# S2 and S4 by pairs of even and of odd chunks, P3's chunks in another order, and A22's third small sum in two halves

## The chip, the cores and the metric

The kernel runs on one core of a Trainium2 chip. The metric is the device time of one launch in microseconds; lower is better. The core has five engines: TensorE (PE) for matmuls, VectorE (DVE), ScalarE (ACT) and GpSimd (POOL) for elementwise work, and SyncE (SP), which here only issues DMAs. POOL issues DMAs too, among them those that add what they carry to what lies at the destination. Each engine works through its own instructions in their order, and waits for the others at semaphores.

## The reference

A causal convolution of 7 taps over 8 sequences of 4096 tokens and 192 channels, with softmaxed weights for each of 8 heads, and after it a feed-forward layer with 2048 hidden channels and a hard-swish:

```python
h = x @ w_in                      # x: 32768 x 192, w_in: 192 x 2048
relu6 = np.clip(h + 3.0, 0.0, 6.0)
g = h * relu6 / 6.0
return (g @ w_out).astype(np.float32)   # w_out: 2048 x 192
```

## The kernel before

The 32768 tokens are taken in 32 blocks of 1024, in two halves of 512. Block 0 is done directly. Blocks 1 to 31 run in a loop of `first_layer` and `second_layer`; what follows is about these.

**First layer.** The hidden channels are 16 chunks of 128; with the two token halves, `g` holds for each of 8 chunk numbers c four tiles of 128 x 512: A11 and A22 (written in the first eight steps, n = 0 to 7) and A21 and A12 (n = 8 to 15). In each step TensorE makes h from a split of inputs and weights in three parts (line 511), ScalarE scales it (L523) and makes the clipped factor (L302), and VectorE multiplies (L306, the "gate").

**Second layer.** `g @ w_out` is a product of 2 x 2 blocks, done with seven products P1 to P7 in place of eight, after sums of the A blocks: S1 = A21 + A22, S2 = S1 - A11, S3 = A11 - A21, S4 = A12 - S2. Four of the seven are split once more in the same way into "small" products, on quarters of the chunks and tokens: x11 and x12 are the even and the odd chunks of the first 256 tokens, x21 and x22 those of the last 256. Their sums are `small_sums` (L600; forms 1 to 4), into the tiles `shared` (for A11), `sums4` (a tile z, for A22), `sums2` (a tile z, for A12) and `s5` (for S1, in the place of A22).

Several sums lie in place of what they come from: S1 lies in A21, S2 in A11, and S4 in the tile s of S3. So each has to wait until the last reader of the old content is through:

- S3 (`third_sum`, `g_sums`, L414): by chunk pairs 0 to 3. Pair 0 on VectorE at n == 9, pair 1 on POOL at n == 11, pairs 2 and 3 on VectorE at the start of the second layer.
- S1 (`add_pair`, L568): a DMA from POOL's queue adds A22 to A21, one pair of chunks after its third_sum.
- S2 (L458 onto g): VectorE subtracts A11 from S1, in place of A11. Its readers are P1 and the small products of P1, which read the even chunks early and the odd chunks of the last 256 tokens last.
- S4 (`negative`, which calls `difference`): ScalarE writes -S2 into the chunk's place in s (L571), and a DMA from POOL's queue adds A12 (L568). The old content, S3, is read by P7; the new one by P3.

TensorE runs four streams of matmuls side by side, each with 32 output rows. Every stream is a list of parts with a cost: 2 for a matmul of 512 columns, 1 for one of 256, 80 in all. `put` and `do` give each matmul and each job of the other engines a time on this scale, and all of them are sorted by it. That sets the order in every engine's queue; it is written out by hand, and nothing is reordered later:

```python
def put(j, cost, fn):
    streams[j].append((clock[j], fn))
    clock[j] += cost

def do(t, fn, *args, **kw):
    streams[3].append((t - 0.5, lambda: fn(*args, **kw)))
```

P7 reads s from 4 to 44, P6 reads S2 from 44 to 60, P3 reads s from 64 to 80, chunk by chunk. In the last block P3 runs by halves of the tokens (`plain_by_halves`), each over all eight chunks.

Between the small products ScalarE copies partial results out of PSUM or within it (lines 740 to 745 from `level_two`, L647 for the rest). Three of those within it are C2, D2 (both copies of B2) and the copies between `a[second]` and `a[fourth]`. `last_sum` negates a small sum of A12 on ScalarE (L571 into z) and adds to it by DMA; `fold_with` adds the parts of P1 on VectorE, and a copy of 96 rows (L647) then puts P1 where P6 is added to it.

Of the kernel before, what the change touches and what calls it, by code (L numbers as in the profile page):

```python
# [8 lines left out]
ALU = mybir.AluOpType  # L9
# [16 lines left out]
def kernel(  # L26
# [8 lines left out]
    nc = tc.nc  # L35
# [10 lines left out]
    D2 = P // 2  # L46
# [8 lines left out]
    NP = NC // 2  # L55
# [32 lines left out]
    for base, dma in ((0, nc.scalar), (D2, nc.sync)):  # L88
        dma.dma_start(
            out=w_sb[base : base + D2],  # L90
            in_=weight.unsqueeze(1).to_broadcast([H, GJ, KC]),
# [126 lines left out]
    for n in range(AHEAD):  # L218
# [8 lines left out]
        out=e_sb[:], in0=w_sb[:], in1=mx[:].to_broadcast([P, KC]), op=ALU.subtract  # L227
# [46 lines left out]
    A11, A21, A12, A22 = (g4[:, :, j] for j in range(4))  # L274
    S2, S1, S4 = A11, A21, A12
# [25 lines left out]
    def relu(r6, h):  # L301
        nc.scalar.activation(r6, h, ACT.Relu, bias=half[:], scale=1.0 / 6.0)  # L302

    def gate(g_, h):

        nc.vector.scalar_tensor_tensor(  # L306
            out=g_, in0=g_, scalar=1.0, in1=h, op0=ALU.min, op1=ALU.mult
        )
# [46 lines left out]
    every = range(NP)  # L355
# [48 lines left out]
    def g_sums(engine, which, slots, width):  # L404

        forms = {
            3: (S3, A11, A21, ALU.subtract),
            2: (S2, S1, A11, ALU.subtract), 4: (S3, A12, S2, ALU.subtract),
        }
        for n in which:  # L410
            o, a, b, op = forms[n]
            for p in slots[::width]:
                r = slice(p, p + width)
                engine.tensor_tensor(out=o[:, r], in0=a[:, r], in1=b[:, r], op=op)  # L414
# [42 lines left out]
    def add(out, x, y, op=ALU.add):  # L457
        nc.vector.tensor_tensor(out=out, in0=x, in1=y, op=op)  # L458
# [13 lines left out]
    def r32(ap):  # L472
        return ap.bitcast(F32R)
# [16 lines left out]
    y_own, y_other, pools, sums4 = [], [None], [], []  # L490
# [8 lines left out]
    def first_layer(i, jobs):  # L499

        slots = {}

        def both(n):
            return psum[:, 2 * slots[n] : 2 * slots[n] + 2]

        def mms(n, part, start=False, stop=False):
            group, c = divmod(n, NP)
            for s in range(K3):
                for k in range(2):
                    r = slice(k * D2, (k + 1) * D2)  # L510
                    nc.tensor.matmul(  # L511
                        out=psum[:, 2 * slots[n] + k], lhsT=r32(w_in_parts[part][r, c, s]),
                        rhs=r32(y_other[0][r, part, s] if group else y_own[part][r, s]),
                        start=start and s == 0, stop=stop and s == K3 - 1,
                        skip_group_check=True,
                    )

        def begin(n):
            slots[n] = free_slots.pop(0)
            mms(n, HIGH, start=True)  # L520
            mms(n, LOW)
            if n + 1 < count:
                nc.scalar.mul(both(n), both(n), 4097.0)  # L523
            else:
                lower, upper = (psum[:, 2 * slots[n] + k] for k in range(2))
                nc.scalar.mul(lower, lower, 4097.0)
                nc.vector.tensor_scalar(
                    out=upper, in0=upper, scalar1=4097.0, scalar2=None, op0=ALU.mult
                )

        def end(n):
            group, c = divmod(n, NP)
            mms(n, MIX, stop=True)
            to = g4[:, c, 1:3] if group else g4[:, c, 0::3]
            relu(to, both(n))
            gate(to, both(n))
            free_slots.append(slots[n])

        count = 2 * NP
        begin(0)  # L540
        begin(1)
        for job in jobs.get(-1, ()):
            job()
        for n in range(count):
            if n == count - 3:
                begin(n + 2)
            end(n)
            if n < count - 3:
                begin(n + 2)
            for job in jobs.get(n, ()):  # L550
                job()
            if n < NP and n % 2:
                small_sums(shared, A11, (3, 2, 4), nc.gpsimd, every[n - 1 : n + 1])
            if n == NP - 1:
                sums4[:] = [pools[0].tile([P, NP, N], F32, name="z4", tag="own")]
                nc.sync.dma_start(out=four_parts(sums4[0])[0], in_=four_parts(A22)[2])
            if n == NP + 1:
                third_sum(0, nc.vector)
                add_pair(0)
                adding(four_parts(sums4[0])[0], four_parts(A22)[3])  # L560
                small_sums(sums4[0], A22, (3,), nc.gpsimd)
            if n == NP + 3:
                third_sum(1)
                add_pair(1)
                small_sums(sums4[0], A22, (2,), nc.gpsimd)

    def adding(out, x):
        nc.gpsimd.dma_start(out=out, in_=x, accum_op=ALU.add)  # L568
# [5 lines left out]
    def pair_of(p):  # L574
        return slice(2 * p, 2 * p + 2)

    def third_sum(p, engine=nc.gpsimd):
        g_sums(engine, (3,), every[pair_of(p)], 2)

    def add_pair(p):  # L580
        adding(S1[:, pair_of(p)], A22[:, pair_of(p)])

    TH = N // 2
    halves = slice(0, TH), slice(TH, N)

    def four_parts(x):
        return [x[:, c::2, t] for t in halves for c in range(2)]

    def small_sums(to, x, which, engine=nc.gpsimd, r=every):

        r = slice(r[0], r[-1] + 1)
        x11, x12, x21, x22 = four_parts(x[:, r])
        s1, s2, s3, s4 = four_parts(to[:, r])
        forms = {
            1: (s1, x21, x22, ALU.add), 2: (s2, x22, s3, ALU.subtract),
            3: (s3, x11, x21, ALU.subtract), 4: (s4, x12, s2, ALU.subtract),
        }
        for n in which:
            o, p, q, op = forms[n]
            engine.tensor_tensor(out=o, in0=p, in1=q, op=op)  # L600
# [17 lines left out]
    def second_layer(i, between):  # L618
        last = i + 1 == NB
        ours = [free_slots.pop(0) for _ in range(3)]  # L620
        x_, b, y_, c, a, _ = (psum[:, 2 * n + k] for n in ours for k in range(2))
# [3 lines left out]
        s5 = A22  # L625
        copy = nc.scalar.copy
        m = slice(0, DH)
        lo, hi = halves
# [7 lines left out]
        A2, E2, C2, B2, D2 = f[first, lo], f[second, hi], h[first, lo], h[second, hi], h[third, hi]  # L636
# [9 lines left out]
        def do(t, fn, *args, **kw):  # L646
            streams[3].append((t - 0.5, lambda: fn(*args, **kw)))  # L647
# [7 lines left out]
        def plain(j, bank, n, q, chunks, start=False):  # L655
            x, w = prod[n]
            x = S3 if x is None else x
            for k, ch in enumerate(chunks):
                put(j, 2, lambda ch=ch, k=k: matmul(
                    j, bank[rows(j)], w_out[:, ch, w, q * QS : (q + 1) * QS], x[:, ch],  # L660
                    start and k == 0,
                ))
# [27 lines left out]

        def plain_by_halves(j, n, q, t):
            w = prod[n][1]
            for ch in every:
                put(j, 1, lambda ch=ch: matmul(
                    j, ends[t][rows(j), halves[t]], w_out[:, ch, w, q * QS : (q + 1) * QS],
                    S3[:, ch, halves[t]], ch == 0,
                ))
# [25 lines left out]
        def p3(q):  # L723
            if last:
                plain_by_halves(q, 3, q, 0)
                plain_by_halves(q, 3, q, 1)
            else:
                plain(q, b, 3, q, every)

        class Fourth:  # L730
            def __getitem__(self, at):
# [82 lines left out]
        do(25.5, copy, out=p1[third], in_=b[second])  # L814
        do(20, copy, out=B2, in_=A2)
        do(31.9, copy, out=C2, in_=B2)
        do(32.2, copy, out=D2, in_=B2)
        do(12, copy, out=a[second], in_=a[fourth])
        do(34, copy, out=a[fourth], in_=a[second])
        do(40, lambda: copy(out=p2(second, hi), in_=C2))  # L820
# [13 lines left out]
        do(7, small_sums, sums2, A12, (3, 2), nc.vector)  # L834
        do(7, small_sums, sums4[0], A22, (4,), nc.vector)
        do(7, small_sums, sums2, A12, (1,), nc.vector)
        for r, t, when in (
            (slice(0, 4), lo, 28.5), (slice(4, 6), lo, 28.6),
            (slice(0, 4), hi, 32.5), (slice(4, 6), hi, 32.6),
        ):  # L840
            do(when, lambda r=r, t=t: add(S2[:, r, t], S1[:, r, t], A11[:, r, t], ALU.subtract))
        do(32, tiles)
        do(36.03, fold_with, p1)
        do(36.07, small_sums, s5, S1, (3,), nc.vector)
        do(36.1, g_sums, nc.vector, (2,), every[6:], 2)
        do(36.2, small_sums, s5, S1, (2,), nc.vector)
        do(36.05, fold_with, p4, 2)
        do(40 if last else 38.7, copy, out=b[m], in_=p1)
        do(21, last_sum, sums2, A12)
        do(36.3, small_sums, s5, S1, (1, 4), nc.vector)  # L850
        for n, t in zip(range(0, NP, 2), (36.3, 39, 41, 48.3)):
            do(t, negative, slice(n, n + 2))
        do(56.5, lambda: copy(out=late["p7"], in_=c[m]))
        do(60.2, lambda: add(late["u3"], b[m], late["p7"]))
        for t in halves:
# [82 lines left out]
    with tc.manual_schedule():  # L938
# [4 lines left out]
            out=c_sb[:], in0=e_sb[:], in1=sm[:].to_broadcast([P, KC]), op=ALU.mult  # L943
# [14 lines left out]
        b = take()  # L958
        for _ in range(3):

            nc.tensor.matmul(
                out=psum[:, b], lhsT=zeros[:, 0:P], rhs=zeros[:], start=True, stop=True
# [58 lines left out]
        n = 3  # L1021
# [146 lines left out]
```

## Time and profile before

| what | value |
|---|---|
| median of 3 runs | 2228.58 us (2228.41 to 2228.99) |
| profiled execution | 2228.83 us |
| its span, first to last instruction | 2227.1 us |
| granted TensorE clock, of full speed | 0.999 |
| busy: TensorE, VectorE, ScalarE, POOL | 2214.7, 2022.1, 1740.9, 1180.5 us |
| second layer's matmuls on s (x3024) | 721.6 us busy, 3.1 us of idle before them, 2.8 of it for the DMA into s |
| ScalarE's wait for VectorE ahead of the negation of z (x31) | 46.9 us |

A row of a timeline gives the start in us from the start of the span, the duration in us, the engine, the line, the operation, what it writes and reads by the program's names with the shape, how many instructions are merged in the row, and in brackets the idle time of the engine before it and what ended it. A row of the chain gives start, duration and what: the chain is followed back from the last instruction to whatever released it. A row of the view of one line gives the count and then the minimum, median and maximum of the duration in ns.

### The profile page before, as it was taken

How to read it: one execution, taken by the hardware profiler on the slowest of the kernel's cores; microseconds unless marked ns; L12 is line 12 of the kernel's file. 1: busy time of each engine (PE TensorE's matmuls, PEld its weight loads, DVE VectorE, ACT ScalarE, POOL GpSimd, SP SyncE). 2: the span in 40 equal slices, each digit the busy share in tenths (PEclk: the TensorE clock that was granted, in tenths of full speed). 3: DMA queues.
4: the chain of work that ended last, by engine and by line, in shares of the span. 5: the costliest groups of instructions: out<-in, count | busy, mean ns of one | idle time of the engine just before them, and what ended most of it. 6: DMA issues, size and time to landing. Idle time of an engine off the chain costs nothing.

```text
span 2227.1 us, 55364 instructions
## 1 busy us (share of the span) xinstructions
PE 2214.7 (99%) x22984; PEld 1461.4 (66%) x22984; DVE 2022.1 (91%) x2014; ACT 1740.9 (78%) x2391; POOL 1180.5 (53%) x1002
## 2 busy tenths in 40 slices
PE   9999999999999999999999999999999999999998
PEld 5466666667666666666676666666666666667765
DVE  8899999999899999999999999999999999999977
ACT  7478787787877878877878778787778787787875
POOL 2456545565544556445555546554456545565544
PEclk9999999999999999999999999999999999999999
DMA  6277788777778777787777887777877788777776
GB/s 157 61 134 137 145 150 150 135 140 146 147 138 157 135 142 147 143 157 131 139 146 148 143 151 135 146 143 141 159 130 139 143 150 151 139 137 143 137 141 113
DMA packets 353308, 313.20 MB, mean 141 GB/s; under 512 B 212480, under 2 KB 265216, under 8 KB 353056
## 3 DMA queue, kind: packets, MB, share of 16 engines
q0 software_dynamic: 114976, 234.46, 58.8%
q1 hardware_dynamic: 236840, 74.93, 16.8%
q8 instruction: 180, 2.95, 0.6%
q14 instruction: 72, 0.59, 0.1%
q10 hardware_dynamic: 1240, 0.27, 0.1%
HBM read 31.72 MB, written 25.17 MB: 26 GB/s over the span
## 4 chain that ended last, share of the span: by engine, by line
PE 92%; DMA 4%; ACT 2%; DVE 1%; issue 0%; SPq 0%; DVEq 0%; ACTq 0%
PE psum L511 46%; PE psum L650 43%; DMA s<-g 4%; PE psum L296 2%; PE psum L341 2%; ACT s L571 1%; ACT psum L647 0%; DMA x<-in_x_dram 0%; ACT shared L823 0%; ACT psum L740 0%; ACT y_own L476 0%; ACT shared L822 0%; DVE z L600 0%; DVE g L306 0%; DVE shared L458 0%
## 5 line engine op out<-in xcount | busy, mean ns | idle before, releaser
L650 PE MATMUL psum<-g,w_out 128*32 128x512 f32 (+1 forms) x5968 | 827.5, 503 | 0.6 <-ACT psum L647 0.6
L650 PE MATMUL psum<-s,w_out 128*32 128x512 f32 (+1 forms) x3024 | 721.6, 586 | 3.1 <-DMA s<-g 2.8
L306 DVE SCALAR_TENSOR_TENSOR g<-g,psum 128x1024 f32<-128x1024 f32 (+1 forms) x528 | 618.9, 1186 | 102.9 <-ACT g L302 102.6
L302 ACT ACTIVATE g<-psum,half 128x1024 f32<-128x1024 f32 (+1 forms) x528 | 565.4, 1088 | 6.0 <-PE psum L511 5.2
L511 PE MATMUL psum<-y_own,w_in 64*128 64x512 f32 x4464 | 523.3, 389 | 0.0
L511 PE MATMUL psum<-y_other,w_in 64*128 64x512 f32 x4464 | 516.0, 386 | 0.0
L523 ACT ACTIVATE psum<-psum 128x1024 f32<-128x1024 f32 x465 | 468.7, 1008 | 48.0 <-PE psum L511 45.3
L650 PEld LDWEIGHTS psum<-g,w_out 128*32 128x32 f32 x5968 | 337.4, 110 | 246.0 <-issue 110.6
L511 PEld LDWEIGHTS psum<-y_own,w_in 64*128 64x128 f32 x4464 | 413.5, 184 | 117.7 <-issue 26.0
L511 PEld LDWEIGHTS psum<-y_other,w_in 64*128 64x128 f32 x4464 | 418.1, 184 | 87.8
L600 POOL TENSOR_TENSOR shared<-g,shared 128x256 f32<-128x256 f32 x248 | 356.7, 1438 | 80.2 <-DVE g L306 48.6
L1058 DVE SCALAR_TENSOR_TENSOR y<-x,c_sb,y 128x1536 f32<-128x1536 f32 x186 | 335.4, 1803 | 1.5 <-ACT y L1056 1.3
L650 PE MATMUL psum<-g,w_s 128*32 128x256 f32 x1488 | 283.2, 380 | 0.3 <-ACT shared L744 0.3
L568 POOL DMA_DIRECT2D s<-g x124 | 148.5, 1199 | 231.4 <-ACT s L571 223.1
L650 PE MATMUL psum<-z,w_s 128*32 128x256 f32 x992 | 232.4, 380 | 0.0
L650 PEld LDWEIGHTS psum<-s,w_out 128*32 128x32 f32 x3024 | 193.8, 109 | 58.5 <-issue 15.9
L650 PE MATMUL psum<-z,w_out 128*32 128x256 f32 x992 | 231.4, 380 | 0.0
L568 POOL DMA_DIRECT2D g<-g x124 | 150.4, 1276 | 151.0 <-PE psum L511 86.7
L600 POOL TENSOR_TENSOR shared<-g 128x256 f32<-128x256 f32 x124 | 91.9, 741 | 167.9 <-DVE g L306 167.9
L650 PEld LDWEIGHTS psum<-g,w_s 128*32 128x32 f32 x1488 | 134.5, 110 | 61.6 <-ACT shared L744 14.4
L647 ACT COPY psum<-psum 32x512 f32<-32x512 f32 (+1 forms) x186 | 82.9, 446 | 117.0 <-PE psum L650 113.1
L266 POOL DMA_DIRECT2D y_other<-y_own x90 | 48.1, 534 | 237.8 <-PE psum L650 237.8
(116 smaller groups left out, 2975.2 us busy)
## 6 DMA issues: line engine op xcount, KB each, us to landing
y_other<-y_own POOLq DMA_DIRECT2D x180, 384.0 KB, 8.0
g<-g POOLq DMA_DIRECT2D x124, 512.0 KB, 5.3
s<-g POOLq DMA_DIRECT2D x124, 512.0 KB, 7.8
z<-g POOLq DMA_DIRECT2D x62, 512.0 KB, 7.4
out_dram<-shared SPq DMA_DIRECT2D x378, 64.0 KB, 4.5
x<-in_x_dram SPq DMA_DIRECT2D x53, 388.5 KB, 5.6
z<-g SPq DMA_DIRECT2D x31, 512.0 KB, 3.3
stage<-in_moe_w_in_dram SPq DMA_DIRECT2D x16, 192.0 KB, 4.7
```

Of the source, the lines that this page charges most:

```text
L266: dma.dma_start(out=to[D2:P], in_=part[0:D2])
L296: nc.tensor.matmul(out=psum[:, b], lhsT=w[r], rhs=src, start=start, stop=stop, skip_group_check=onto,)
L302: nc.scalar.activation(r6, h, ACT.Relu, bias=half[:], scale=1.0 / 6.0)
L306: nc.vector.scalar_tensor_tensor(out=g_, in0=g_, scalar=1.0, in1=h, op0=ALU.min, op1=ALU.mult)
L341: lambda p=p: nc.tensor.matmul(out=bank[j * QS : (j + 1) * QS, tokens], lhsT=w_out[:, p, w, cols], rhs=x[:, p, tokens], start=(first and p ...
L511: nc.tensor.matmul(out=psum[:, 2 * slots[n] + k], lhsT=r32(w_in_parts[part][r, c, s]), rhs=r32(y_other[0][r, part, s] if group else y_own[ ...
L523: nc.scalar.mul(both(n), both(n), 4097.0)
L568: nc.gpsimd.dma_start(out=out, in_=x, accum_op=ALU.add)
L600: engine.tensor_tensor(out=o, in0=p, in1=q, op=op)
L647: streams[3].append((t - 0.5, lambda: fn(*args, **kw)))
L650: nc.tensor.matmul(out=out, lhsT=w, rhs=x, start=start, stop=True, tile_position=(0, j * QS), skip_group_check=True,)
L1058: jobs.append(lambda k=k: nc.vector.scalar_tensor_tensor(out=y[:], in0=x[:, :, k : k + N], scalar=c_sb[:, k : k + 1], in1=y[:], op0=ALU.mu ...
```

## The change

- A22's third small sum (form 3 of `sums4`), which POOL did in one at n == 9, is done in two halves: chunks 0 to 3 at n == 7, chunks 4 to 7 at n == 9. At n == 11 POOL's second small sum goes ahead of `add_pair(1)`.
- S2 was made in five sums: chunks 0 to 3 and 4 to 5 by token halves, chunks 6 and 7 whole. Now it is made in four, by the chunk pairs 0 2, 4 6, 1 3 and 5 7 in this order, each over all tokens.
- S4's four negations with their DMAs go by the pairs 0 2, 1 3, 4 6, 5 7 in place of 0 1, 2 3, 4 5, 6 7, at 30.5, 36.3, 42.1 and 44.2 in place of 36.3, 39, 41 and 48.3. So in ScalarE's queue the first negation now stands ahead of copy C2 (31.9).
- The copy D2 goes from 32.2 to 45.
- P3 takes the chunks in the order 0 2 1 3 4 6 5 7, in the last block too.
- The third sum of `s5` goes from 36.07 to 36.15, behind S2's last pair.

The number of matmuls and their order by size and stream are the same.

```diff
             if n == NP - 1:
                 sums4[:] = [pools[0].tile([P, NP, N], F32, name="z4", tag="own")]
                 nc.sync.dma_start(out=four_parts(sums4[0])[0], in_=four_parts(A22)[2])
+                small_sums(sums4[0], A22, (3,), nc.gpsimd, every[:4])
             if n == NP + 1:
                 third_sum(0, nc.vector)
                 add_pair(0)
                 adding(four_parts(sums4[0])[0], four_parts(A22)[3])
-                small_sums(sums4[0], A22, (3,), nc.gpsimd)
+                small_sums(sums4[0], A22, (3,), nc.gpsimd, every[4:])
             if n == NP + 3:
                 third_sum(1)
+                small_sums(sums4[0], A22, (2,), nc.gpsimd)
                 add_pair(1)
-                small_sums(sums4[0], A22, (2,), nc.gpsimd)
...
+    in_fours = 0, 2, 1, 3, 4, 6, 5, 7
+    chunk_pairs = [slice(n, n + 3, 2) for n in (0, 1, 4, 5)]
...
-            for ch in every:
+            for ch in in_fours:
                 put(j, 1, lambda ch=ch: matmul(
                     j, ends[t][rows(j), halves[t]], w_out[:, ch, w, q * QS : (q + 1) * QS],
...
-                plain(q, b, 3, q, every)
+                plain(q, b, 3, q, in_fours)
...
-        do(32.2, copy, out=D2, in_=B2)
+        do(45, copy, out=D2, in_=B2)
...
-        for r, t, when in (
-            (slice(0, 4), lo, 28.5), (slice(4, 6), lo, 28.6),
-            (slice(0, 4), hi, 32.5), (slice(4, 6), hi, 32.6),
-        ):
-            do(when, lambda r=r, t=t: add(S2[:, r, t], S1[:, r, t], A11[:, r, t], ALU.subtract))
+        for r, when in zip(chunk_pairs, (28.5, 32.5, 28.6, 36.1)):
+            do(when, lambda r=r: add(S2[:, r], S1[:, r], A11[:, r], ALU.subtract))
         do(32, tiles)
         do(36.03, fold_with, p1)
-        do(36.07, small_sums, s5, S1, (3,), nc.vector)
-        do(36.1, g_sums, nc.vector, (2,), every[6:], 2)
+        do(36.15, small_sums, s5, S1, (3,), nc.vector)
         do(36.2, small_sums, s5, S1, (2,), nc.vector)
...
-        for n, t in zip(range(0, NP, 2), (36.3, 39, 41, 48.3)):
-            do(t, negative, slice(n, n + 2))
+        for r, t in zip(chunk_pairs, (30.5, 36.3, 42.1, 44.2)):
+            do(t, negative, r)
```

## The prediction

> **What bounds the kernel now.** I read the page first, for the busiest engine and for the chain that ended last, then that chain in order of time, because only it says which waits move the end.
>
> ```profile
> PE 2214.7 (99%) x22984; PEld 1461.4 (66%) x22984; DVE 2022.1 (91%) x2014; ACT 1740.9 (78%) x2391; POOL 1180.5 (53%) x1002
> PE 92%; DMA 4%; ACT 2%; DVE 1%; issue 0%; SPq 0%; DVEq 0%; ACTq 0%
> 99.82 32.93 PE psum L511 x288
> ...
> 413.30 1.21 DVE s L414
> ...
> 419.55 0.37 ACT shared L744
> ...
> 419.97 22.68 PE psum L650 x167
> ...
> 1112.75 1.06 ACT s L571
> ...
> 1114.11 9.17 DMA s<-g
> ...
> 1123.32 1.93 PE psum L650 x16
> 1125.25 32.97 PE psum L511 x288
> 1158.22 35.21 PE psum L650 x289
> ...
> 2150.28 32.97 PE psum L511 x288
> ```
>
> TensorE is busy for 99% of the span. One block of the loop is 288 matmuls of the first layer (L511, 32.97 us) and then the second layer (L650). A block without a visible wait takes 32.97 + 35.21 = 68.18 us. From the first L511 stretch (99.82) to the last (2150.28) lie 30 blocks in 2050.46 us, 68.35 each: so all visible waits of these 30 blocks are worth 30 x 68.35 - 30 x 68.18 = 5.1 us. The chain names two kinds. Mostly it is the last chunk pair of S4, which P3 waits for: ScalarE writes -S2 (L571, 1112.75), POOL's DMA adds A12 and lands 9.17 us after its issue at 1114.11, and sixteen matmuls later the block ends. Once, at 413 to 420, it is VectorE's third sum, then ScalarE's copy L744. What remains inside the 35.21 us shows only beside the engines of one block. Below is the block whose second layer starts at 1089.7; a part of a stream that costs 1 there (I call it a unit) lasts about 0.43 us: ScalarE's copies of units 16 and 20, both waiting for TensorE, start at 1096.89 and 1098.60.
>
> ```profile
> 1101.98 0.38 PE L650 MATMUL psum<-z,w_s 128*32 128x256 f32 x1
> ...
> 1102.31 0.41 PE L650 MATMUL psum<-g,w_s 128*32 128x256 f32 x2
> 1105.83 0.40 PE L650 MATMUL psum<-z,w_out 128*32 128x256 f32 x1
> 1109.09 4.24 PE L650 MATMUL psum<-g,w_out 128*32 128x256 f32 x40
> 1096.89 0.72 ACT L742 COPY psum<-psum 32x256 f32<-32x256 f32 x2 [1.20 <-PE psum L650]
> 1098.60 0.34 ACT L647 COPY psum<-psum 32x256 f32<-32x256 f32 x1 [1.00 <-PE psum L650]
> 1100.42 1.06 ACT L571 ACTIVATE z<-z 128x1024 f32<-128x1024 f32 x1 [1.48 <-DVE z L600]
> 1101.89 0.36 ACT L744 COPY shared<-psum 32x256 f32<-32x256 f32 x1
> 1102.88 0.37 ACT L743 COPY z<-psum 32x256 f32<-32x256 f32 x1
> 1105.07 1.28 ACT L647 COPY psum<-psum 32x256 f32<-32x256 f32 x3
> 1107.04 1.05 ACT L571 ACTIVATE s<-g 128x1024 f32<-128x1024 f32 x1
> 1108.12 0.59 ACT L647 COPY psum<-z 96x512 f32<-96x512 f32 x1
> ...
> 1093.08 3.78 DVE L414 TENSOR_TENSOR s<-g 128x1024 f32<-128x1024 f32 x2
> 1099.16 2.36 DVE L600 TENSOR_TENSOR z<-g,z 128x1024 f32<-128x1024 f32 x2
> 1102.58 3.56 DVE L458 TENSOR_TENSOR g<-g 128x1024 f32<-128x1024 f32 x4
> ...
> 1085.02 3.35 POOL L600 TENSOR_TENSOR z<-g 128x1024 f32<-128x1024 f32 x1
> 1087.38 3.34 POOL L414 TENSOR_TENSOR s<-g 128x1024 f32<-128x1024 f32 x1
> 1091.02 1.19 POOL L568 DMA_DIRECT2D g<-g  x1 [0.30 <-POOL s L414]
> 1091.77 2.86 POOL L600 TENSOR_TENSOR z<-g,z 128x1024 f32<-128x1024 f32 x1
> ...
> L414 DVE TENSOR_TENSOR s<-g x93: 1210/1225/3420, 124.6 to 2189.1; 128x1024 f32<-128x1024 f32 x93
> ```
>
> This is the part the change works on. VectorE's pair of third sums (L414) takes 3.78 us, though a sum of this shape takes 1.22 us at the median of 93 and 1.21 at least. The first of the two is the one held up: 3.78 - 1.14 - 1.22 leaves some 1.4 us, and POOL's second small sum ends at 1091.77 + 2.86 = 1094.63, inside it. Everything behind it on VectorE is late by the same 1.4 us, and so ScalarE idles 1.48 us at 1100.42 for a sum of VectorE, with all its copies queued behind. Two of these copies hold TensorE: L744 ends at 1102.25 and TensorE goes on at 1102.31; of the three L647 copies behind 1105.07 the first two (C2 and D2) are of the size that takes 0.34 at 1098.60, so D2 ends near 1105.78, and TensorE goes on at 1105.83.
>
> **Part one, POOL's sums.** The third small sum of A22 now runs half at n == 7 and half after add_pair(0), and the second small sum goes ahead of add_pair(1). What is left behind 1085.02 is half a sum, POOL's third_sum and the second sum. With whole durations this is 1085.02 + 1.7 + 3.34 + 2.86 = 1092.9; with the pitch of the rows (1087.38 - 1085.02 = 2.36 for a whole one) it is 1085.02 + 1.2 + 2.36 + 2.36 = 1090.9, to which the overlap with the DMA issue may add one. Both lie ahead of VectorE's 1093.08. So the pair takes 1.22 + 1.14 and ends 1.4 us earlier (1095.4), and the sum for which ScalarE waits ends at about 1099.0. Queued behind the moved second sum is add_pair(1): issued 1 to 2 us later, it lands near 1098, ahead of the first S2 sum that reads it, at 1101.2.
>
> ```profile
> 1077.61 3.01 POOL L600 TENSOR_TENSOR shared<-g,shared 128x256 f32<-128x256 f32 x2 [0.37 <-POOL shared L600]
> 1081.59 1.23 DVE L414 TENSOR_TENSOR s<-g 128x1024 f32<-128x1024 f32 x1
> 1084.41 1.22 DVE L306 SCALAR_TENSOR_TENSOR g<-g,psum 128x1024 f32<-128x1024 f32 x1 [0.46 <-ACT g L302]
> ```
>
> The moved half starts at 1080.62, when POOL's last row of the first layer ends, and ends 1.2 to 1.7 us later, at 1081.8 to 1082.3; VectorE wants its first third_sum at 1081.59. If that one is held up like the pair above, it loses 0.2 to 0.7 us, and 0.46 us of idle two sums later takes it up. Bounds: 0 to 0.24 us in 31 blocks, 0 to 7 us; I take 0, since TensorE is two chunks behind there. The Trainium skill (SBUF — State Buffer, Who interferes with whom) has it that a VectorE instruction with two SBUF inputs and a GpSimd instruction reading SBUF lock each other out for the whole instruction, the earlier one winning. The held pair of L414 agrees; by that rule the moved half does hold up this sum in every block, and the total would lie in the same 0 to 7 us.
>
> **Part two, ScalarE's queue.** Today the chain from L743 to the end of D2 is 1102.88 to 1105.78. L743 waits for unit 28, which by the rows of units 16 and 20 is served at 1098.60 + 8 x 0.43 = 1102.03. With the last sum's negation at 99.0 to 100.1 and L744, L647 behind it (0.39 + 0.39 + 0.6), ScalarE is free at 1101.5: L744 no longer holds TensorE, and L743 starts at 1102.03, 0.85 us earlier. Then comes the added wait: the first S4 negation (30.5) stands ahead of copy C2 (31.9), for 1.08 us; D2 (0.37) leaves. So C2 ends 0.85 - 0.71 = 0.14 us earlier, and TensorE, for which C2 is now the last, goes on 0.08 to 0.14 us earlier at this place. Take 0.1: 31 x 0.1 = -3.1 us. The bounds are wide: without any gain on VectorE it would be +0.71 per block, and with both holds gone (0.33 us of delay at 1102.31, after 1101.98 by the pace, and as much again at 1105.83) about -0.65. Queued behind the negation are also L745, the second negation and the 96-row copy that P6 waits for: 1108.12 becomes 1107.98, ahead of TensorE's 1109.09 at P6, so its cover stays 0.4 us.
>
> **Part three, S2 by pairs.** Five sums become four of 1.22 us: what was 3.56 + 1.22 is now 4.88, nothing to speak of. The order is what counts. The second sum, chunks 4 and 6, now needs add_pair(2) and add_pair(3); these issue 1.4 us earlier, with their third sums.
>
> ```profile
> 1096.44 2.43 POOL L568 DMA_DIRECT2D g<-g  x2 [1.82 <-DVE s L414]
> DMA to landing us min/median/max: 5.1/6.2/7.3
> DMA to landing us min/median/max: 5.0/7.8/9.6
> ```
>
> The first landing row is of these two, so the later one, issued near 1097.2, lands at 1104.5, and after the change near 1103.1. VectorE reaches this sum at 1102.4, waits 0.7 us, and ends chunks 1 and 3 at 1103.1 + 1.22 + 1.14 = 1105.5. ScalarE wants them for the second negation at 1106.9. The cover is 1.4 us; a landing 9.6 us after its issue, the most of any S4 addition (the second landing row), uses it up and costs 0.9. I put +1.2 us over the kernel for a few late blocks; bounds 0 and 31 x 0.9 = 28. The third sum of s5, now behind S2's last pair, only changes places with it.
>
> **Part four, S4 and P3.** The last negation moves from 1112.75 to about 1110.8 and its DMA issues near 1112.1, 2 us earlier; the three before it move 2 to 3 us earlier too. Even at 9.6 us to landing it is there at 1121.7, and P3 wants it, as the sixth chunk now instead of the seventh of 0 to 7 but at the same unit 76, at about 1122.9 (1123.32, where TensorE now goes on, less a wait of some tenths). So the waits on S4 go, and with the earlier VectorE the one at 413 too: -5.1 us. What is late next is C2 (part two). In the last block P3 runs by halves and wants the last pair at unit 70:
>
> ```profile
> 2214.63 0.59 PE L650 MATMUL psum<-g,w_out 128*32 128x256 f32 x2
> 2216.23 0.42 PE L650 MATMUL psum<-s,w_out 128*32 128x256 f32 x3 [1.00 <-DMA s<-g]
> ```
>
> The next step was due 0.2 us after 2214.63; 2216.23 is 1.4 us late, and 2 us earlier covers it: -1.4 us.
>
> **The sum.** -5.1 - 1.4 - 3.1 + 1.2 = -8.4 us. The profiled execution took 2228.83 us (span 2227.1); the median of the runs, 2228.58, is 0.25 lower. That gives 2220.4; I say 2220.5, -0.36%. A difference under 0.2% (4.5 us) can't be told from none by a measurement of this kernel.
>
> **Rivals.** First, slower: the queue is paid and the gain does not come. If POOL's second sum still lies over VectorE's pair, ScalarE's chain starts as late as now and C2 ends 0.71 us later in each block: +22 - 6.5 = +15.5 us, 2244. It decides from the point where POOL's sum ends after about 1093.7, 0.6 us into VectorE's pair; against it stands 1090.9 to 1092.9 above, for it that the trace's spans of POOL overlap and are rough. Second, no change: VectorE's wait for chunks 4 and 6 takes the place of the one removed. POOL's three add_pairs now start closer together (add_pair(1) later, the others earlier), and if the last lands some 1.7 us later than I have it, each block loses about 0.3 us at P6 and the 8.4 us are eaten: 2228. The two landings of 5.1 and 7.3 us, the later one queued behind the earlier, speak for it. Third, more: if C2 comes in time after all, both holds go, 31 x 0.65 = 20 in place of 3.1, with 6.5 from S4: 2202. The 1.08 us of the negation ahead of C2 speak against it.
>
> **How the numbers follow.** Forecast 0.60, slower 0.17, no change 0.14, more 0.09. Faster by over 0.2% is 0.69, within it 0.14, slower 0.17. The forecast's own range is 2214 to 2224 from the bounds of the moved half and of the late landings. For eight in ten the range takes in the second rival and the near part of the first (a partial gain on VectorE), and leaves out the far end of the first and most of the third: 2212 to 2233.
>
> **What would show it.** Right: L414's pair near 2.4 us, ScalarE's idle ahead of the negation of z under 0.3 us, no wait of L650 on the DMA into s, blocks of 68.0 to 68.1 us. Wrong: L414 still with a maximum at 2.6; TensorE's release at unit 36 later than 16.1 us after the second layer's start; a wait of VectorE's L458 on the DMA into g of over 1.4 us; a hold of TensorE by the gate in the first layer.

## The result, and the profile after

| | before | after |
|---|---|---|
| median | 2228.63 us, 7 runs (2227.93 to 2229.71) | 2220.66 us, 7 runs (2220.51 to 2221.03) |
| ratio after to before | | 0.9963, 95% interval 0.9952 to 0.9975 |
| span of the profiled execution | 2227.1 us | 2218.7 us |

The change makes the kernel 8 us faster; 2220.5 had been forecast. In the changed kernel the lines behind L554 have moved by up to 3, so L653 is the matmul of the second layer, L572 the negations, L569 POOL's DMAs, L650 the single copies, and L743 to L748 the copies of `level_two`.

The first view of after is the page's busy line and the rows of the chain of waits (start, us, what), one block and the last one:

```profile
PE 2201.0 (99%) x22984; PEld 1481.5 (67%) x22984; DVE 1985.3 (89%) x1983; ACT 1741.4 (78%) x2391; POOL 1182.7 (53%) x1033
99.86 32.93 PE psum L511 x288
...
1086.10 12.27 PE psum L653 x120
...
1100.58 1.06 ACT s L572
1101.66 0.34 ACT psum L650
...
1102.05 19.16 PE psum L653 x129
1121.21 32.97 PE psum L511 x288
...
2142.81 32.97 PE psum L511 x288
...
2194.49 1.23 DVE g L458
2195.72 1.15 DVE g L603
```

From the first L511 stretch to the last lie 2142.81 - 99.86 = 2042.95 us, 7.5 less than before in the same 30 blocks; from the last stretch to the end of the span it is 75.89 in place of 76.82, 0.9 less. No DMA into s is in the chain any more. In its place the chain leaves TensorE in every block: ScalarE's negation for S4 (1100.58) stands ahead of the copy C2, and TensorE goes on at 1102.05, behind that copy.

The second view is the timelines of POOL, VectorE and ScalarE in the same block (its second layer starts at 1086.0), with the count of all third sums of VectorE (minimum, median, maximum in ns):

```profile
1076.90 1.30 POOL L603 TENSOR_TENSOR z<-g 128x512 f32<-128x512 f32 x1
...
1084.80 3.39 POOL L603 TENSOR_TENSOR z<-g,z 128x1024 f32<-128x1024 f32 x1
...
1077.91 1.36 DVE L414 TENSOR_TENSOR s<-g 128x1024 f32<-128x1024 f32 x1
...
1089.39 2.35 DVE L414 TENSOR_TENSOR s<-g 128x1024 f32<-128x1024 f32 x2
...
1100.00 2.36 DVE L458 TENSOR_TENSOR g<-g 128x1024 f32<-128x1024 f32 x2 [1.33 <-PE psum L653]
L414 DVE TENSOR_TENSOR s<-g x93: 1202/1218/1398, 124.6 to 2180.2; 128x1024 f32<-128x1024 f32 x93
1095.30 1.06 ACT L572 ACTIVATE z<-z 128x1024 f32<-128x1024 f32 x1
...
1100.58 1.06 ACT L572 ACTIVATE s<-g 128x1024 f32<-128x1024 f32 x1
1101.66 0.91 ACT L650 COPY psum<-psum 32x256 f32<-32x256 f32 x2
...
1103.26 1.05 ACT L572 ACTIVATE s<-g 128x1024 f32<-128x1024 f32 x1
...
1108.49 0.34 ACT L743 COPY psum<-psum 32x256 f32<-32x256 f32 x1
```

The pair of third sums that took 3.78 us takes 2.35, and the maximum of all 93 is 1.40 us where it was 3.42: POOL's second small sum ends at 1088.19 (1084.80 + 3.39), ahead of the pair at 1089.39. Only the sum at 1077.91 still starts under a sum of POOL, the moved half, which ends at 1078.20; it takes 1.36 us. ScalarE's negation of z has no idle time of note ahead of it (1.48 before). From 1098.8 to 1110.8 ScalarE goes from one row to the next without a pause, and the copy L743, which the small products of P5 wait for, stands near the end of that queue.

The third view is the list of waits (total us, times, longest us), the rows of TensorE on the single copies (C2 among them) and of VectorE ahead of its S2 sums, and behind them the answer on the last addition into S1 in the same block (its issue, and the time to its landing):

```profile
PEld psum L653 <- ACT psum L650: 24.2, 32, 0.8
DVE g L458 <- PE psum L653: 30.9, 25, 1.9
DVE g L458 <- DMA g<-g: 9.6, 5, 2.5
PE psum L653 <- ACT psum L650: 9.0, 31, 0.3
...
L569 POOL DMA_DIRECT2D g<-g x1: 1706/1706/1706, 1092.1 to 1092.1; - x1
DMA to landing us min/median/max: 7.9/7.9/7.9
```

By the names in this list VectorE waits mostly for TensorE, which reads the old content of S2. The times say otherwise. In the block shown the last addition into S1 lands at 1100.0 (1092.1 + 7.9), which is when VectorE starts its second S2 sum (1100.00). By the trace this sum starts 0.08 us after that landing in every one of the 30 blocks, from 13.2 to 15.3 us after the second layer's start. TensorE runs the same in every block up to here, and the earliest start shows that its part of the wait is over by 13.2 us. So VectorE waits for the DMA, whatever name the profile puts there.

### The profile page after: what moved, and what is told of

The parts are those of the page before. It is cut to its first block, busy times and chain, and to the rows that moved or that the text cites. A ratio compares the mean times of both kernels' runs of the same rounds, so it can differ in the third digit from the quotient of the medians.

```text
span 2218.7 us, 55332 instructions
## 1 busy us (share of the span) xinstructions
PE 2201.0 (99%) x22984; PEld 1481.5 (67%) x22984; DVE 1985.3 (89%) x1983; ACT 1741.4 (78%) x2391; POOL 1182.7 (53%) x1033
## 4 chain that ended last, share of the span: by engine, by line
PE 93%; ACT 4%; issue 1%; DVE 0%; DMA 0%; SPq 0%; DVEq 0%; ACTq 0%
PE psum L511 46%; PE psum L653 44%; PE psum L296 2%; PE psum L341 2%; ACT s L572 1%; ACT shared L650 1%; ACT z L744 1%; ACT shared L744 1%; ACT psum L650 1%; DMA x<-in_x_dram 0%; DVE shared L458 0%; DVE g L603 0%; SPq L100 0%; DVE shared L464 0%; DVE g L458 0%
## 5 line engine op out<-in xcount | busy, mean ns | idle before, releaser
L653 PE MATMUL psum<-g,w_out 128*32 128x512 f32 (+1 forms) x5968 | 825.7, 503 | 0.0
L653 PE MATMUL psum<-s,w_out 128*32 128x512 f32 (+1 forms) x3024 | 713.7, 586 | 0.0
L511 PE MATMUL psum<-y_own,w_in 64*128 64x512 f32 x4464 | 523.3, 389 | 0.0
L511 PE MATMUL psum<-y_other,w_in 64*128 64x512 f32 x4464 | 516.0, 386 | 0.0
L653 PEld LDWEIGHTS psum<-g,w_out 128*32 128x32 f32 x5968 | 338.5, 110 | 245.5 <-issue 111.4
L511 PEld LDWEIGHTS psum<-y_own,w_in 64*128 64x128 f32 x4464 | 413.5, 184 | 117.7 <-issue 26.0
L511 PEld LDWEIGHTS psum<-y_other,w_in 64*128 64x128 f32 x4464 | 418.1, 184 | 87.8
L603 POOL TENSOR_TENSOR shared<-g,shared 128x256 f32<-128x256 f32 x248 | 357.6, 1442 | 88.4 <-DVE g L306 57.0
L653 PE MATMUL psum<-g,w_s 128*32 128x256 f32 x1488 | 283.3, 379 | 0.3 <-DVE g L603 0.3
L569 POOL DMA_DIRECT2D s<-g x124 | 148.4, 1197 | 214.1 <-PE psum L653 124.2
L653 PE MATMUL psum<-z,w_out 128*32 128x256 f32 x992 | 235.1, 380 | 9.0 <-ACT psum L650 9.0
L569 POOL DMA_DIRECT2D g<-g x124 | 181.8, 1530 | 103.9 <-DVE s L414 103.9
L653 PE MATMUL psum<-z,w_s 128*32 128x256 f32 x992 | 227.5, 379 | 0.0
L653 PEld LDWEIGHTS psum<-s,w_out 128*32 128x32 f32 x3024 | 192.8, 110 | 51.2 <-issue 14.0
L458 DVE TENSOR_TENSOR g<-g 128x1024 f32<-128x1024 f32 x124 | 149.0, 1222 | 43.6 <-PE psum L653 30.9
L603 POOL TENSOR_TENSOR shared<-g 128x256 f32<-128x256 f32 x124 | 91.9, 741 | 170.3 <-DVE g L306 170.3
L650 ACT COPY psum<-psum 32x512 f32<-32x512 f32 x186 | 82.9, 446 | 116.4 <-PE psum L653 113.3
```

What stands on the lines that cost most here:

```text
L511: nc.tensor.matmul(out=psum[:, 2 * slots[n] + k], lhsT=r32(w_in_parts[part][r, c, s]), rhs=r32(y_other[0][r, part, s] if group else y_own[ ...
L653: nc.tensor.matmul(out=out, lhsT=w, rhs=x, start=start, stop=True, tile_position=(0, j * QS), skip_group_check=True,)
```

## The experiments

All ratios are to the kernel before, on the same chip, with their 95% intervals. "The changed kernel" is after.

**POOL's part alone.** The kernel before with this and nothing else:

```diff
             if n == NP - 1:
...
+                small_sums(sums4[0], A22, (3,), nc.gpsimd, every[:4])
             if n == NP + 1:
...
-                small_sums(sums4[0], A22, (3,), nc.gpsimd)
+                small_sums(sums4[0], A22, (3,), nc.gpsimd, every[4:])
             if n == NP + 3:
                 third_sum(1)
+                small_sums(sums4[0], A22, (2,), nc.gpsimd)
                 add_pair(1)
-                small_sums(sums4[0], A22, (2,), nc.gpsimd)
```

> The kernel before with part one alone: A22's third small sum in two halves, the second small sum ahead of add_pair(1); S2, S4, P3 and the copies as before. Theory (POOL's sum holds up VectorE's pair of third sums, and the late ScalarE copies L744 and D2 hold TensorE): the pair takes 2.4 us in place of 3.8, ScalarE's idle of 1.48 us ahead of the negation of z goes, L743 is bound by unit 28 of TensorE, and with no negation ahead of C2 the copy D2 ends near 15.2 us after the second layer's start, ahead of unit 36 (15.5). Both holds go: 0.6 us per block, some -19 us, about 2209; the waits of P3 stay, or shrink a little. Rival (the gain of 8 us comes from S4's earlier addition alone, VectorE's pair is off the path): 2228, within 0.2% of before.

2209.88 us (2206.79 to 2212.35), ratio 0.9916 (0.9901 to 0.9930): 11 us better than the whole change. The chain and the waits of this kernel (here L651 is the second layer's matmul):

```profile
1012.41 34.61 PE psum L651 x289
...
PEld psum L651 <- DMA s<-g: 6.5, 9, 1.8
PE psum L651 <- DMA s<-g: 2.6, 5, 1.3
```

A block without a wait takes 32.97 + 34.61 = 67.58 us, 0.6 less than before: both holds of TensorE that the prediction named are gone. A few blocks still wait for S4.

**Everything but POOL's part.** The changed kernel with the diff above taken back.

> The changed kernel without part one: POOL's small sums of A22 as they were, S2, S4, P3 and D2 as changed. Theory: VectorE's pair takes 3.8 us again, ScalarE is as late as before and has the first S4 negation (1.08 us) in place of D2 (0.37) ahead of C2, so TensorE goes on 0.7 us later in each of 31 blocks: +22 us, less 6.5 us for the waits of P3 that are gone: about 2244. Rival (S4's earlier addition is the gain and the queue price is hidden): 2221 to 2223.

2249.04 us (2248.89 to 2249.15), ratio 1.0092 (1.0077 to 1.0107). Two rows of its chain, a block apart, its third sums and its wait on C2 (L652, L649 here):

```profile
1045.64 1.06 ACT s L571
1114.52 1.06 ACT s L571
L414 DVE TENSOR_TENSOR s<-g x93: 1210/1225/3435, 124.6 to 2208.8; 128x1024 f32<-128x1024 f32 x93
PE psum L652 <- ACT psum L649: 18.4, 32, 0.6
```

The third sum is held as before (maximum 3.4 us), and a block takes 1114.52 - 1045.64 = 68.88 us, 0.70 more than before. So the edits of S2, S4, P3 and D2 lose time by themselves, 20 us, and in the whole change they give back 11 of the 19 us that POOL's part brings.

**Which half of POOL's part.** First the two halves of the third sum alone (second sum left behind add_pair(1)), then the second sum moved alone (third sum left in one).

> The kernel before, with A22's third small sum in two halves and nothing else; add_pair(1) stays ahead of POOL's second small sum. Theory A, VectorE's first third_sum of the pair is held to about 1.1 us after the end of POOL's small sum (4.92 and 6.0 us after the second layer's start before): the small sum now ends near 3.7, the pair's first takes 1.4 to 1.5 us in place of 2.65, and the chain of ScalarE behind it has 0.28 us to spare: 2210 to 2212. Rival B, the sums have to be apart altogether and the move of the second sum is what matters: 2225 or more.

> The kernel before, with POOL's second small sum ahead of add_pair(1) and nothing else; the third small sum stays in one. Theory A: by the pitch of POOL's rows the second sum runs from 0.05 to 3.4 us after the second layer's start, VectorE's pair starts at 3.35: held by 0.1 us at most, 2210. Rival B, with whole durations (3.4 and 3.4 and 2.9 us, one behind the other from -4.7) it ends at 5 as before: no change, 2228.

2206.67 us (2206.46 to 2208.38), ratio 0.9901 (0.9886 to 0.9915), and 2206.92 us (2206.57 to 2207.80), ratio 0.9901 (0.9885 to 0.9918). Either is enough, and 3 us or more better than theory A had it; both together bring nothing more (2209.88, its runs from 2206.79). With the halves alone, POOL's and VectorE's timelines show how the hold works:

```profile
1080.32 2.88 POOL L601 TENSOR_TENSOR z<-g,z 128x1024 f32<-128x1024 f32 x1
1082.83 2.60 DVE L414 TENSOR_TENSOR s<-g 128x1024 f32<-128x1024 f32 x2
```

POOL's sum ends at 1083.20 and VectorE's pair, begun at 1082.83, takes 2.60, which is 0.25 more than 2.35. The overlap is 0.37 us. In the kernel before the overlap was 1.55 us (1093.08 to 1094.63) and the pair 1.43 longer than 2.35: VectorE loses the overlap less a tenth of a microsecond, and no more.

**The first negation behind C2.** In the changed kernel:

```diff
-        for r, t in zip(chunk_pairs, (30.5, 36.3, 42.1, 44.2)):
+        for r, t in zip(chunk_pairs, (35, 36.3, 42.1, 44.2)):
```

> The changed kernel with the first S4 negation at 35 in place of 30.5: behind the copies C2 and a[fourth], ahead of L745. Theory: C2 ends 1.08 us earlier and holds TensorE no more at unit 36 (0.5 us per block); the copy that P6 waits for stands where it did, at 18.9 us after the second layer's start, and TensorE, now early, meets it at 18.7: 0.2 us come back there. Net about -0.3 us per block, -9 us: 2212. P3's waits stay away, with 3 us of cover. Rival (what holds TensorE at unit 36 isn't C2): no change from 2220.7.

2219.18 us (2218.61 to 2219.29), ratio 0.9957 (0.9941 to 0.9974), a miss: 1.5 us better than the changed kernel where 9 had been expected. TensorE is 0.5 us earlier than in the changed kernel from unit 36 to unit 78 and has lost that again at the block's end. The timelines of ScalarE and TensorE show where:

```profile
1108.00 0.34 ACT L743 COPY psum<-psum 32x256 f32<-32x256 f32 x1
1108.40 0.40 PE L653 MATMUL psum<-g,w_s 128*32 128x256 f32 x1
...
1119.54 0.62 PE L653 MATMUL psum<-s,w_out 128*32 128x512 f32 x3
1119.64 1.02 PE L653 MATMUL psum<-g,w_out 128*32 128x512 f32 x2
```

L743 ends at 1108.34, and the first small product behind it starts at 1108.40, one step (0.43 us) later than its stream was due. The other three streams don't stop for it. The stream of P5 stays one step behind them to the end: after the last step of P3 (s, x3) two of its steps (g, x2) are left in place of one, and only there does the hold cost time.

**The first two negations behind the copies for P1.**

```diff
-        for r, t in zip(chunk_pairs, (30.5, 36.3, 42.1, 44.2)):
+        for r, t in zip(chunk_pairs, (35, 39, 42.1, 44.2)):
```

> As the run before it, with the second S4 negation also moved, from 36.3 to 39, behind the copy of P1 that P6 waits for. Theory: that copy comes 0.5 to 1 us earlier, both holds are gone, -0.55 us per block: about 2203 to 2205. Rival (the copy is bound by VectorE's fold, not by the queue): as the run before it, within 2 us.

2237.14 us (2236.49 to 2237.56), ratio 1.0038 (1.0023 to 1.0053), a miss with the wrong sign. Its longest hold of a matmul, and a wait of ScalarE that the run before doesn't have:

```profile
PEld psum L653 <- ACT psum L743: 27.5, 30, 1.3
ACT psum L650 <- DVE z L458: 18.4, 30, 1.5
```

The rival named the mechanism, though not the time. The second negation had stood ahead of the 96-row copy and had filled the time until VectorE's fold was done. Now ScalarE sits idle there instead, 0.6 us in each block, with the same number of negations still to do. So its queue comes later from there on, and L743 with it: it starts 23.0 us after the second layer's start in place of 22.5 in the run before. The stream of P5 is 0.56 us later from its first small product to the block's end, and so is the block: 68.58 us without another wait, after 68.02.

**Two copies moved behind L743.** The kernel with the first negation at 35, and:

```diff
-        do(44, lambda: copy(out=p2(first, lo), in_=A2))
-        do(44, lambda: copy(out=p2(second, lo), in_=E2))
+        do(52, lambda: copy(out=p2(first, lo), in_=A2))
+        do(52, lambda: copy(out=p2(second, lo), in_=E2))
```

> The kernel with the first negation behind C2 (2219.2 us), and ScalarE's two copies of A2 and E2 (0.36 us each), which stand ahead of the last S4 negation, moved from 44 to 52, behind the copy that the small products of P5 wait for. Theory A, ScalarE's queue is full from the first negation to that copy, and a copy that comes 0.45 us late costs one stream one pass of TensorE in each block: the copy comes 0.7 us earlier, the pass comes back, 30 x 0.45 = 13.5 us less, 2205 to 2206, a clean block of 67.6 us. Rival B, the lost pass at the end of the block comes from VectorE's sums for P5 or from the parts of y for the next first layer: no change, 2219, a block of 68.03 us.

2206.65 us (2206.41 to 2206.98), ratio 0.9898 (0.9884 to 0.9913): close to theory A. ScalarE's and TensorE's timelines, for the same two places:

```profile
1101.17 0.34 ACT L743 COPY psum<-psum 32x256 f32<-32x256 f32 x1
...
1113.47 0.62 PE L653 MATMUL psum<-s,w_out 128*32 128x512 f32 x3
1113.56 0.59 PE L653 MATMUL psum<-g,w_out 128*32 128x512 f32 x1
```

L743 starts 21.7 us after the second layer's start (1079.48) in place of 22.5, and all four streams end together. The block is 67.58 us, as with POOL's part alone, and now without waits on S4.

**POOL's part with an earlier last negation.** The kernel of the first experiment with the same two copies at 52 and the last negation at 46 in place of 48.3.

> The kernel before with POOL's part alone (2209.9 us), and in it the same two copies from 44 to 52 and the last S4 negation from 48.3 to 46. Theory A: the last negation comes some 1.5 us earlier and the copy for P5 no later than 22.1 us after the second layer's start, so nothing is lost on TensorE, and the waits of P3 on S4 that were left (2.6 us in 30 blocks, about 1 us in the last) go: 2206 to 2207, all blocks 67.58. Rival B, the negation ahead of the copy for P5 costs what it costs in the changed kernel: 2209.9 - 3.5 + 13.5 = 2220.

2207.24 us (2206.28 to 2208.01), ratio 0.9901 (0.9886 to 0.9916). The time is that of theory A, its reason isn't: the waits on S4 stay. The runs of the first experiment reach down to 2206.79, so a gain over it isn't shown either.

```profile
PEld psum L651 <- DMA s<-g: 7.1, 9, 1.6
PE psum L651 <- DMA s<-g: 3.0, 4, 1.1
```

The last addition issues 1.7 us earlier than in the first experiment (21.9 after 23.6 us from the second layer's start, medians) and lands at 32.4 after 32.3. Here are the answers on POOL's DMAs into s in one block: in the first experiment the last addition, then the two last of this kernel (the second line of each is the time from issue to landing):

```profile
L569 POOL DMA_DIRECT2D s<-g x1: 1200/1200/1200, 1103.5 to 1103.5; - x1
DMA to landing us min/median/max: 8.9/8.9/8.9
```

```profile
L569 POOL DMA_DIRECT2D s<-g x2: 1206/1350/1495, 1101.6 to 1102.5; - x2
DMA to landing us min/median/max: 9.8/10.3/10.8
```

Issued 1.7 us earlier against the block's start, the last takes 1.9 us longer to land (10.8 after 8.9). What all kernels share is another distance: from the issue of the first addition to the landing of the last it is 14.2 to 14.6 us, both taken as medians over the blocks: in the kernel before 18.7 to 33.2, in the changed one 15.9 to 30.3, in this one 17.9 to 32.4.

**The first negation earlier, the last left.** The kernel of the first experiment with `(35, 39, 41, 48.3)` in place of `(36.3, 39, 41, 48.3)`.

> The kernel before with POOL's part alone (2209.9 us) and in it S4's first negation from 36.3 to 35, the last one left at 48.3. In the eight kernels so far the last S4 addition lands 14.4 to 14.6 us after the first one is issued, and the time of its own issue (21.6 to 24.4 us after the second layer's start) doesn't show in it. Theory A, the four additions are one chain that the first negation starts: it is issued 1.0 us earlier, the last lands at 31.3 in place of 32.3 us at the median, 32.3 in place of 33.3 at most, and the waits of P3 go: 2206.5 us, all blocks 67.58. Rival B, the last addition's own issue sets its landing: the waits stay, 2209.9.

2213.69 us (2213.26 to 2213.78), ratio 0.9930 (0.9915 to 0.9945). On the landings theory A holds: the first addition issues 0.67 us earlier (17.20), the last, issued later than before (24.23), lands 0.5 us earlier (31.80, at most 32.5), and of the waits for a DMA into s one is left, 0.3 us of a weight load. On the time it misses, because of ScalarE's queue once more:

```profile
1015.21 34.90 PE psum L651 x291
PEld psum L651 <- DVE shared L458: 12.0, 30, 0.4
ACT psum L648 <- DVE z L458: 16.4, 30, 0.6
...
1108.34 1.76 DVE L1082 TENSOR_TENSOR y_own<-y,y_own 128x1536 fp32r<-128x1536 f32 x1 [0.60 <-ACT y_own L476]
1110.13 0.69 DVE L458 TENSOR_TENSOR shared<-psum,shared 96x512 f32<-96x512 f32 x1
```

The second layer takes 34.90 us where the first experiment's chain has 34.61: 0.29 us more in every block. TensorE loses most of it where P3 begins, waiting for VectorE's sum that empties the bank P3 writes to (1110.13). That sum stands in VectorE's queue behind L1082, which prepares the next block's inputs and waits for ScalarE's L476; and L476 comes 0.6 us later than in the first experiment. The cause is the one of the run with the first two negations moved: the negation at 36.3 had filled ScalarE's time until VectorE's fold was done, and with it gone ScalarE is idle there, 16.4 us in 30 blocks, where the first experiment has no such wait.

**P3's order.** The changed kernel with `in_fours = every`, so that P3 takes its chunks from 0 to 7.

> The changed kernel with P3 taking its chunks in the order 0 to 7 again. Theory A: P3 wants the pair 1 3 one chunk earlier and the pair 5 7 at unit 74 in place of 76, 0.86 us earlier, and the S4 additions land 2 to 3 us ahead of that: no change, 2220.7, no wait of a matmul on the DMA into s but in the last block at most. Rival B, P3's order is what took the waits on S4 away: they come back, 2224 to 2226.

2220.79 us (2220.65 to 2221.35), ratio 0.9962 (0.9947 to 0.9977), a block 68.08: in the changed kernel P3's order does nothing.

**S2's order.** The changed kernel with S2's sum of chunks 1 and 3 ahead of that of 4 and 6:

```diff
-        for r, when in zip(chunk_pairs, (28.5, 32.5, 28.6, 36.1)):
+        for r, when in zip(chunk_pairs, (28.5, 32.5, 32.6, 36.1)):
```

> The changed kernel with S2's sum of chunks 1 and 3 ahead of that of chunks 4 and 6. Theory A: VectorE's wait of 1.7 us for the addition of S1 into chunks 6 and 7 lies behind the sum that the second negation wants, the two late blocks (0.68 us together) go and nothing else moves, because ScalarE's queue sets the rest: 2220.0, all blocks 68.08. Rival B, VectorE's wait is what keeps the whole chain of ScalarE late: earlier by 0.4 us per block, 2208 to 2212.

2219.76 us (2219.14 to 2219.83), ratio 0.9956 (0.9940 to 0.9973): 0.9 us below the changed kernel's median, as theory A had it. In the changed kernel two blocks were late; this is the chain in the later one, and then in this kernel at the same place:

```profile
1782.80 19.62 PE psum L653 x129
```

```profile
1733.79 32.97 PE psum L511 x288
1801.86 32.98 PE psum L511 x288
```

In the changed kernel the stretch of TensorE behind C2 is 19.62 us there and 19.16 in other blocks; with S2's order changed the block is 1801.86 - 1733.79 = 68.07, like all others.

**The best.** The changed kernel with the first negation at 35, the two copies at 52 and S2's order of the last run.

> The two that came out best put together: the changed kernel with the first negation behind C2, the copies of A2 and E2 at 52, and S2's chunks 1 and 3 ahead of 4 and 6. The two late blocks of the kernel without the last edit (0.62 and 0.81 us) go: 2206.65 - 1.4 = 2205.2 us, all blocks 67.58. If the late blocks had another cause than the addition of S1 into chunks 6 and 7: 2206.6.

2204.98 us (2204.89 to 2205.12), ratio 0.9891 (0.9877 to 0.9906). It beats the kernel before by 23 us and the changed one by 16.

```profile
1011.45 34.61 PE psum L653 x289
```

## Why the prediction was right

The sum was -5.1 - 1.4 - 3.1 + 1.2 = -8.4 us; the span fell from 2227.1 to 2218.7, which is 8.4. That the two agree so closely is partly luck: the terms give 6.9 us for the 30 blocks and 1.5 for the last one, measured are 7.5 and 0.9, and the two differences cancel. By its steps:

- **POOL's sums (part one): right.** VectorE's pair takes 2.35 us (2.36 predicted), and with POOL's part taken out it is held again. Of the moved half it was said that it may hold VectorE's first third sum, 0 to 7 us over the kernel, with 0 taken: the row at 1077.91 has 1.36 us in place of 1.23, and the first layer stays at 32.97 us, so nothing is lost by it. Both rows agree with the rule of the Trainium skill (SBUF — State Buffer, Who interferes with whom): the pair takes 3.78 us with POOL's sum over it and 2.35 without, and the first sum is held under the moved half. What wasn't seen is that one half of this part would do.
- **ScalarE's queue (part two): right.** A clean block is 68.08 us after 68.18, the 0.1 us of the prediction, and the wait for C2 (24.2 and 9.0 us in the rows quoted) is what is late next. The third rival, both holds gone, is what POOL's part gives alone (0.60 us a block). The objection to it, the negation ahead of C2, was true: it is what holds TensorE there. But taking it away brought 1.5 us alone and 14 with the two copies moved as well, because the copy for P5 (L743) stands behind it in the same queue; the prediction followed that queue only as far as P6.
- **S2 by pairs (part three): right in kind, its sizes off.** VectorE waits for the addition into chunks 6 and 7 in every block, as the prediction and its second rival had it. The landing is 14.0 us after the second layer's start at the median where 13.4 had been taken, so the wait is 1.45 us at the median in place of 0.7. Over 1.4 us had been named as a sign that the prediction is wrong, and 16 of the 30 blocks have it. It does no harm in most: chunks 1 and 3 are done at 1102.36 in the block shown, 0.9 us ahead of the second negation (1103.26). Only in two blocks, with landings at 15.1 and 15.3 us, is that cover used up; they cost 0.68 us together, after 1.2 predicted.
- **S4 and P3 (part four): the gain right, its reason not.** The waits on S4 went. The text has the last landing 2 us earlier because its own issue is 2 us earlier; it is 2.9 us earlier because the first of the four additions is issued 2.8 us earlier. Two runs show it: an earlier last issue left the landing where it was, an earlier first one moved it. P3's order had no part in it.
- **The last block: mis-sized.** 0.9 us in place of 1.5 with its share of C2. The chain there now goes over VectorE's last S2 pair and s5's sums (L458 at 2194.49, L603 behind it) before TensorE's last stretch, so the edit said to only "change places" may be what is missing. That was not tried by itself.
- **The slower rival** was priced at 2244; with POOL's part out it came to 2249. The 0.70 us a block agree with its 0.71; it left out five late blocks (3.0 us together), in four of which the negation waits for VectorE's S2, and that the last block gains nothing.

## What to carry to other kernels

A change made of several parts can be faster and still contain a part that loses: here one moved sum on POOL brings 21 us, the whole change 8, and only running the parts alone shows it. When an instruction is to go earlier in a full queue, follow the queue to the next copies that the matmuls wait for, and move behind them something that nobody waits for yet. Look too at what the instruction covers where it stands: two of the misses above moved a negation out of a gap in which ScalarE then sat idle. For transfers that go one behind the other in one queue, look at when the first starts. And where an instruction waits for two things, compare its start with the end of each, block by block, before you believe the name that the profile gives.

## What was not expected of the hardware

- Four additions by DMA of 128 x 1024 values, issued 1 to 3 us apart on POOL's queue, land some 3 us apart: the first of a block about 5 us from its issue, the last 8.9 to 10.8 in the answers above. From the first issue to the last landing it is 14.2 to 14.6 us at the median whether the last is issued 4.0 or 7.0 us behind the first. In all these runs each is issued before the one ahead of it has landed.
- A sum of VectorE that starts while POOL's sum runs ends about 1.1 us after it, so it is held for the overlap less a tenth: 0.13 us with 0.29 us of it, 0.25 with 0.37, 1.43 with 1.55.
- Four streams of matmuls side by side can slide against each other by one step of 0.43 us without any loss that shows, until the block's end, where all four have to be through.
